# Idle transposes at the start, later and re-spread weight widening, and a scale ahead of the clamp, in a fused attention and mixer kernel on one core

## The chip, the cores and the metric

The kernel runs on one core of a Trainium2 chip. The metric is the device time of one execution in microseconds, taken as the median of several runs. The profile is one more execution, followed instruction by instruction. TensorE is called PE (its weight loads PEld), VectorE DVE, ScalarE ACT, GpSimd POOL, and the engine that issues most DMAs SP.

## The reference

Three layers in a row, on 4 batches of 576 tokens of 512 numbers (8 heads of 64), with weights that come in as 64-bit floats:

```python
q_p, k_p = phi(q_s), phi(k_s)                 # phi(x) = exp(h - max h)/sqrt(m), h = x @ omega.T - |x|^2/2
kv = einsum('bhsm,bhsd->bhmd', k_p, v); z = sum(k_p, axis=2)
x = einsum('bhsm,bhmd->bhsd', q_p, kv) / (einsum('bhsm,bhm->bhs', q_p, z)[..., None] + 1e-6)
h = maximum(x.T @ w_tok1, 0) @ w_tok2         # mixing over tokens
u = x + h.T
x = u + maximum(u @ w_ch1, 0) @ w_ch2         # 512 -> 1536 -> 512
u = x + real(fft(fft(x, axis=1), axis=2))
out = u + maximum(layernorm(u) @ w_ch1b, 0) @ w_ch2b   # 512 -> 2048 -> 512
```

## The kernel before

**Products.** Every product of full precision is three PE products of rounded parts (high by high, low by high, high by low). The program order of every engine is written out by hand, so an instruction that waits holds everything behind it on its engine, and a DMA that waits holds everything behind it on its queue.

**Attention** (`attention`, L781) runs in 72 slots, numbered n from 0, and seven more that finish; `order` (L691) holds one half tile of keys or of queries for each. Slots 0 to 9 are keys alone, 10 to 60 alternate keys and queries (so the last keys are in slot 60), and 61 to 71 are queries alone. In a slot PE makes six projections (`project`, L506); DVE takes their maximum (`feature`, L520); ACT makes the exponentials. Three slots later PE adds keys into the sums (`kv_add`, L540, eight products) or transposes queries (`turn`, L565, four). Five slots later it forms numerators (`numer`, L582, eight) that DVE divides (L595 to L602), and seven slots later it transposes the result (`turn_x`, L616). The mixing over tokens (`tok_mix`, L667 with 15 products and L680 with six, added by DVE in L683) is let in piece by piece once a batch is complete. SP loads the tile of a slot six slots ahead (`load`, L478 and L483), and ACT and POOL (keys of the first tiles also DVE) split it into parts four slots ahead (`split_in`, L493 and L494). Projections take their PSUM bank from four that rotate (`bank("A")`); the sums of keys take two that rotate (`bank("H")`).

**Widening** (`widen`, L319) turns a chunk of 64-bit weights into two 32-bit parts: a load into `stg` (L330), then DVE's clamp (`take`, L341), low bits (`rest`, L352), `size` (L356), `high` (L360), `low` (L364), `unit` (L368) and `scaled` (L372), with one ACT multiplication (`scale`, L348) between clamp and `size`. There are 32 chunks: four short ones for the mixing over tokens (640 and 576 columns), then 12 slabs and 16 halves of 1024 columns, which are stored to DRAM (`kept`) and fetched again where they are used. Two sets of buffers alternate, so the load of chunk i+2 overwrites `stg` of chunk i and waits for its `low`.

**Pacing** (`Side`, L202). `weave` (L383) puts the steps of all chunks in one list, each with a price in us of DVE (6.38 for a chunk of 1024). At the end of each slot `side.step(budget)` adds a budget to a credit (at most 4.6 is saved) and issues steps while the credit covers them. Loads and stores are put off by four slots (`side.later`), or are issued at once where a step needs them (`side.flush`). Budgets before: none in slots 0 and 1, 0 in slots 2 to 5, 1.2 in 6 to 9, 0.45 in 10 to 35, 1.2 from 36 on. After attention the channel blocks (`mlp`, L864) call `side.step` once per step of 24 PE products (L776 up, L898 down) with 3.9 in the first block, 1.2 in the second and 4.3 after; there the loads and stores go through POOL's queue without delay. ACT's `relu` (L860) and DVE's low part of it (L861) stand between up and down of a step, with the up product of the next step in between.

## Time and profile before

| what | us |
|---|---|
| median of 3 runs | 954.33 (954.07 to 955.66) |
| the profiled execution | 953.26 |
| its span, first to last instruction | 951.2 |
| PE busy in the span | 931.4 |
| DVE busy | 644.2 |
| ACT busy | 301.3 |

The span is 2.1 us shorter than the time of the same execution, and that execution is 1.1 us faster than the median. Attention's last piece on PE ends at 211.3 us; the blocks after it fill the rest. A PE that is busy is not always at its peak, because each product is drawn with its latency; where the text prices PE work it uses the distance from one start to the next.

### The profile page before, as it was taken

To read this page: it belongs to the slowest core of one execution; us is meant where nothing else is said; L and a number is where in the kernel's file an instruction comes from. 1 tells how busy PE (TensorE), PEld (TensorE's weight loads), DVE (VectorE), ACT (ScalarE), POOL (GpSimd) and SP (SyncE) were. 2 spreads that over 40 slices of the span, in tenths; PEclk is the share of its full clock that TensorE was granted. 3 is DMA by queue.
4 is the path that set the end of the run, shared out by engine and by line. 5 is a ranking of instruction groups with operands and counts; after the bars stand their busy time and mean duration, and the time that the engine had idled before them with its cause. 6 is when DMAs were issued, how large, how long until landed. Compare 5 with 4: busy or idle time off the path is not lost.

```text
span 951.2 us, 14064 instructions
## 1 busy us (share of the span) xinstructions
PE 931.4 (98%) x5344; PEld 829.7 (87%) x5344; DVE 644.2 (68%) x1270; ACT 301.3 (32%) x676; POOL 118.8 (12%) x110
## 2 busy tenths in 40 slices
PE   7999998989999999999999999999999999999998
PEld 7999898878889988888888888889899998899986
DVE  5987999985776687877864577667565457533342
ACT  5885765742122222212221212212311113311121
POOL 3353343321120122011000000000000000000000
PEclk9999999999999999999999999999999999999999
DMA  8665464388889386584155348739776756687764
GB/s 272 221 211 178 143 231 173 122 318 320 341 352 418 100 341 217 191 292 167 67 177 216 139 147 270 246 126 359 266 244 234 238 183 221 221 263 257 252 205 160
DMA packets 68257, 216.47 MB, mean 228 GB/s; under 512 B 5600, under 2 KB 14432, under 8 KB 54240
## 3 DMA queue, kind: packets, MB, share of 16 engines
q1 hardware_dynamic: 60992, 172.40, 51.9%
q0 software_dynamic: 7056, 43.06, 12.3%
q8 instruction: 42, 0.69, 0.3%
q14 instruction: 23, 0.19, 0.1%
q10 hardware_dynamic: 144, 0.13, 0.1%
HBM read 169.30 MB, written 42.47 MB: 223 GB/s over the span
## 4 chain that ended last, share of the span: by engine, by line
PE 89%; DVE 9%; ACT 1%; issue 0%; DMA 0%; DVEq 0%; ACTq 0%
PE H L776 22%; PE A L898 16%; PE A L1470 14%; PE H L1457 12%; PE A L1264 7%; PE A L506 4%; PE H L540 2%; PE N L582 2%; DVE mx L520 2%; PE A L667 1%; PE S L1077 1%; DVE cvo L364 1%; PE A L565 1%; PE S L1090 1%; DVE x L598 1%; DVE cvo L372 1%
## 5 line engine op out<-in xcount | busy, mean ns | idle before, releaser
L776 PE MATMUL H<-uh,w 128*128 128x512 f32 (+1 forms) x800 | 215.3, 355 | 2.1 <-DVE x L683 2.1
L776 PEld LDWEIGHTS H<-uh,w 128*128 128x128 f32 x800 | 136.5, 189 | 22.2 <-DVE x L683 2.3
L860 ACT ACTIVATE hh<-H 128x512 fp32r<-128x512 f32 (+1 forms) x92 | 49.0, 533 | 270.7 <-PE H L776 270.5
L776 PE MATMUL H<-ul,w 128*128 128x512 f32 (+1 forms) x304 | 113.7, 374 | 0.4 <-DVE ul L763 0.4
L898 PE MATMUL A<-hh,w 128*128 128x512 f32 (+1 forms) x480 | 108.7, 369 | 0.0
L861 DVE SCALAR_TENSOR_TENSOR hl<-H,hh 128x512 fp32r<-128x512 f32 (+1 forms) x92 | 55.8, 606 | 64.5 <-ACT hh L860 64.3
L1470 PE MATMUL A<-w2t,b 128*128 128x512 f32 x384 | 99.3, 394 | 0.0
L898 PEld LDWEIGHTS A<-hh,w 128*128 128x128 f32 x480 | 84.3, 189 | 15.0
L1457 PE MATMUL H<-b,w1t 128*128 128x384 f32 x480 | 91.5, 336 | 0.0
L1457 PEld LDWEIGHTS H<-b,w1t 128*128 128x128 f32 x480 | 85.0, 188 | 4.0 <-DVE tmp L1501 0.3
L1470 PEld LDWEIGHTS A<-w2t,b 128*128 128x128 f32 x384 | 70.6, 188 | 11.7
L524 ACT ACTIVATE f<-A,mx 128x128 f32<-128x128 f32 x204 | 58.9, 395 | 31.1 <-DVE mx L520 23.4
L776 PEld LDWEIGHTS H<-ul,w 128*128 128x128 f32 x304 | 57.4, 189 | 9.9 <-DVE ul L763 0.8
L898 PE MATMUL A<-hl,w 128*128 128x512 f32 (+1 forms) x240 | 59.2, 369 | 0.0
L1264 PE MATMUL A<-w,hh 128*128 128x512 f32 x192 | 50.5, 395 | 0.0
L520 DVE TENSOR_REDUCE mx<-A 128x4 f32<-128x512 f32 x70 | 47.6, 681 | 3.7 <-ACT f L524 2.2
L898 PEld LDWEIGHTS A<-hl,w 128*128 128x128 f32 x240 | 42.7, 189 | 7.6
L540 PE MATMUL H<-v,f 128*128 128x65 f32 x320 | 40.5, 272 | 0.4 <-ACT f L524 0.4
L540 PEld LDWEIGHTS H<-v,f 128*128 128x128 f32 x320 | 39.4, 193 | 0.8 <-ACT f L524 0.6
L1264 PEld LDWEIGHTS A<-w,hh 128*128 128x128 f32 x192 | 34.6, 189 | 6.1
L360 DVE SCALAR_TENSOR_TENSOR cvo<-cvy,cvo 128x1024 int32<-128x1024 int32 (+2 forms) x32 | 39.3, 1228 | 0.5
L1462 ACT ACTIVATE b<-tmp 128x384 fp32r<-128x384 f32 x16 | 8.4, 525 | 98.1 <-DVE tmp L1523 98.1
(261 smaller groups left out, 1703.4 us busy)
## 6 DMA issues: line engine op xcount, KB each, us to landing
w<-kept SPq DMA_DIRECT2D x60, 1024.0 KB, 6.8
w2t<-kept SPq DMA_DIRECT2D x55, 512.0 KB, 4.9
w1t<-kept SPq DMA_DIRECT2D x48, 512.0 KB, 5.0
stg<-in_wff_dram POOLq DMA_DIRECT2D x16, 1024.0 KB, 6.8
kept<-cvo POOLq DMA_DIRECT2D x13, 1024.0 KB, 7.3
stg<-in_wch_dram SPq DMA_DIRECT2D x9, 1024.0 KB, 6.1
kept<-cvo POOLq DMA_DIRECT2D x16, 512.0 KB, 7.7
kept<-so SPq DMA_DIRECT2D x16, 512.0 KB, 7.7
```

The costliest lines, as they stand in the source:

```text
L360: dve.scalar_tensor_tensor(out=st["h"], in0=st["y"].bitcast(I32), scalar=-0x80000000, in1=st["h"], op0=ALU.bitwise_and, op1=ALU.bitwise_or)
L506: pe.matmul(out=pj[:, p_ * 256:p_ * 256 + 256], lhsT=a[:, c, :], rhs=w, start=(n == 0), stop=(n == 2), skip_group_check=True)
L520: dve.tensor_reduce(out=mx, in_=p4, axis=AX.X, op=ALU.max, negate=True)
L524: act.activation(out=f[:, hh], in_=p4[:, hh], func=AF.Exp, bias=mx[:, hh])
L540: pe.matmul(out=kvp[b, g][:, hh * 65:hh * 65 + 65], lhsT=ft["k", i, g][:, hh, :], rhs=src["v", i, int(off > 0)][:, 4 * g + hh, :], start=( ...
L776: pe.matmul(out=hb[:, 0:n], lhsT=w(a, kk), rhs=u[:, kk, 0:n], start=(c == 0), stop=(c == 11))
L860: act.activation(out=hh, in_=hb[:, 0:n], func=AF.Relu)
L861: dve.scalar_tensor_tensor(out=hl, in0=hb[:, 0:n], scalar=0.0, in1=hh, op0=ALU.max, op1=ALU.subtract)
L898: pe.matmul(out=acc[i][:, 0:cols], lhsT=a[:, cs], rhs=v, start=(n == 0 and c_ == 0), stop=(n == NCH - 1 and c_ == 2))
L1264: pe.matmul(out=acc[t], lhsT=a[:, t * 128:t * 128 + 128], rhs=w, start=(n == 0 and c_ == 0), stop=(n == NFF - 1 and c_ == 2))
L1457: pe.matmul(out=to, lhsT=w[:, a, cs], rhs=v[:, q], start=(start and n == 0), stop=(n == 5), skip_group_check=True)
L1470: pe.matmul(out=acc[t], lhsT=h[n // 2][:, t * 128:t * 128 + 128], rhs=w[:, n % 2], start=(begins and n == 0), stop=(ends and n == 2))
```

## The change

The change has five edits. (1) After `projection()` PE runs 17 transposes of the identity into a bank of tag H before the first slot. (2) The values of a key tile are loaded one key tile later, so the first keys come ahead of values. (3) `scale` is now the first step of a chunk: ACT multiplies the strided words out of `stg` into `cvy` at no price, and DVE then clamps `cvy` in place with bounds that are scaled as well. In `weave` the scale of chunk i+1 is issued right after `size` of chunk i, ahead of `high`, `low` and `unit`; the clamp and the load of chunk i+2 keep their places. The `while` that forces an outstanding load moves from the clamp to `scale`. (4) `side.step` is first called in slot 8 and no longer in slot 2. (5) The budgets are 0 in slots 8 to 11, 0.6 in 12 to 25, 1.1 in 26 to 57, 0.3 in the eight slots 58 to 65 around the end of the keys (`alone` is 61) and 1.2 after; the first channel block gets 4.2 and no longer 3.9.

```diff
--- before.py
+++ after.py
@@ -27,13 +27,14 @@
 BLK = 512
 
 NWB = 3
+IDLE = 17
 NBLK = (NTOK + BLK - 1) // BLK
 
 BLOCKS = [0, NBLK - 1, *range(1, NBLK - 1)]
 
 
 
-SLOT0_US, SLOT1_US, SLOT_US, FIRST_US, SHORT_US, CH_US, FF_US, S_US, SAVED_US = 1.2, 0.45, 1.2, 3.9, 1.2, 4.3, 3.8, 1.6, 4.6
+SLOT0_US, SLOT1_US, ALONE_US, SLOT_US, FIRST_US, SHORT_US, CH_US, FF_US, S_US, SAVED_US = 0.6, 1.1, 0.3, 1.2, 4.2, 1.2, 4.3, 3.8, 1.6, 4.6
 
 
 NP = NFF // 2
@@ -329,30 +330,27 @@
             st["w"] = cv.tile([128, 2048], I32, tag=f"stg{k}", name="stg")
             side.queue.dma_start(out=st["w"][:, 0:2 * n], in_=src)
 
+        def scale():
+            while "w" not in st:
+                side.flush()
+            v = st["w"][:, 0:2 * n].rearrange("p (n w) -> p n w", w=2)
+            st["lw"], st["hw"] = v[:, :, 0], v[:, :, 1]
+            st["y"] = cv.tile([128, 1024], F32, tag=f"cvy{k}", name="cvy")[:, 0:n]
+            act.mul(out=st["y"], in_=st["hw"].bitcast(F32), mul=2.0 ** -112)
+
         def take():
-            while "w" not in st or k in busy:
+            while k in busy:
                 side.flush()
             busy.add(k)
-            v = st["w"][:, 0:2 * n].rearrange("p (n w) -> p n w", w=2)
-            st["lw"], hw = v[:, :, 0], v[:, :, 1]
-            st["y"] = y = cv.tile([128, 1024], F32, tag=f"cvy{k}", name="cvy")[:, 0:n]
             st["o"] = cv.tile([128, 2, 1024], F32R, tag=f"cvo{k}", name="cvo")
             st["h"], st["l"] = (st["o"][:, a, 0:n].bitcast(I32) for a in range(2))
-            dve.tensor_scalar(out=y, in0=hw.bitcast(F32), scalar1=HMAX, scalar2=-HMAX, op0=ALU.min, op1=ALU.max)
-            side.later(scale, 1)
-
-        def scale():
-
-            if "small" not in st:
-                st["small"] = True
-                act.mul(out=st["y"], in_=st["y"], mul=2.0 ** -112)
+            dve.tensor_scalar(out=st["y"], in0=st["y"], scalar1=HMAX * 2.0 ** -112, scalar2=-HMAX * 2.0 ** -112,
+                              op0=ALU.min, op1=ALU.max)
 
         def rest():
-            hw = st["w"][:, 0:2 * n].rearrange("p (n w) -> p n w", w=2)[:, :, 1]
-            dve.tensor_scalar(out=st["l"], in0=hw, scalar1=0x1FF, scalar2=None, op0=ALU.bitwise_and)
+            dve.tensor_scalar(out=st["l"], in0=st["hw"], scalar1=0x1FF, scalar2=None, op0=ALU.bitwise_and)
 
         def size():
-            scale()
             dve.tensor_scalar(out=st["h"], in0=st["y"].bitcast(I32), scalar1=3, scalar2=0x7FFFF000,
                               op0=ALU.logical_shift_left, op1=ALU.bitwise_and)
 
@@ -377,7 +375,7 @@
 
         f = n / 1024
         return (load, lambda: done(st, free)), [
-            (w * f, fn) for w, fn in ((0.68, take), (0.68, rest), (0.69, size), (1.21, high), (1.21, low), (0.69, unit),
+            (w * f, fn) for w, fn in ((0.0, scale), (0.68, take), (0.68, rest), (0.69, size), (1.21, high), (1.21, low), (0.69, unit),
                                       (1.22, scaled))]
 
     def weave(chunks):
@@ -386,13 +384,16 @@
         items = []
         for i, ((_, done), work) in enumerate(chunks):
             if not i:
-                items += [(0.0, chunks[c][0][0]) for c in range(2)] + work[:1]
-            items += work[1:6]
+                items += [(0.0, chunks[c][0][0]) for c in range(2)] + work[:2]
+            items += work[2:4]
             if i + 1 < len(chunks):
                 items.append(chunks[i + 1][1][0])
+            items += work[4:7]
+            if i + 1 < len(chunks):
+                items.append(chunks[i + 1][1][1])
             if i + 2 < len(chunks):
                 items.append((0.0, lambda i=i: side.later(chunks[i + 2][0][0])))
-            items.append(work[6])
+            items.append(work[7])
             items.append((0.0, lambda done=done: side.later(done)))
         return items
 
@@ -478,10 +479,17 @@
         sync.dma_start(out=t, in_=(kt if kind == "k" else qt)[:, i])
         src[kind, i] = t
         if kind == "k":
-            for part, row in enumerate([i] + [NT + c for c, j in enumerate(SPLIT) if j == i]):
-                t = ld.tile([128, H, D + 1], F32, tag="v", name="v", bufs=6)
-                sync.dma_start(out=t.rearrange("p h d -> p (h d)"), in_=va[row])
-                src["v", i, part] = t
+            values(i - 1)
+        if kind == "k" and i == NT - 1:
+            values(i)
+
+    def values(i):
+        if i < 0 or ("v", i, 0) in src:
+            return
+        for part, row in enumerate([i] + [NT + c for c, j in enumerate(SPLIT) if j == i]):
+            t = ld.tile([128, H, D + 1], F32, tag="v", name="v", bufs=6)
+            sync.dma_start(out=t.rearrange("p h d -> p (h d)"), in_=va[row])
+            src["v", i, part] = t
 
     def split_in(kind, i):
         t = src.pop((kind, i))
@@ -783,6 +791,7 @@
         at = {t: order.index(t + (int(t[0] == "q"),)) for t in tiles}
         late = {}
         n_all = len(order)
+        alone = max(n for n, x in enumerate(order) if x[0] == "k") + 1
 
         def at_slot(n, kind):
             return order[n][1:] if 0 <= n < n_all and order[n][0] == kind else None
@@ -828,9 +837,10 @@
             if 0 <= n < n_all:
                 feature(*order[n])
             results(n)
-            if n >= 2:
-
-                side.step(0.0 if n < 6 else SLOT0_US if n < 10 else SLOT1_US if n < 36 else SLOT_US)
+            if n >= 8:
+
+                side.step(0.0 if n < 12 else SLOT0_US if n < 26 else SLOT1_US if n < alone - 3 else
+                          ALONE_US if n < alone + 5 else SLOT_US)
             if fill and (len(fill) > 3 or n % 2 == 0):
                 fill.pop(0)()
             for fn in early[:3]:
@@ -839,6 +849,9 @@
 
     ctx.enter_context(tc.manual_schedule())
     projection()
+    idle = bank("H")
+    for _ in range(IDLE):
+        pe.transpose(idle[:, 0:128], ident, ident)
     side.rest += weave(tok_weights() + [slab(j) for j in range(NCH)]
                        + [w(p_) for p_ in range(NP) for w in (first, second)])
     attention()
```

## Rows read from the trace of the kernel before

**Rows 1.** Page, part 1: busy time, share of the span and instructions of each engine.

```profile
PE 931.4 (98%) x5344; PEld 829.7 (87%) x5344; DVE 644.2 (68%) x1270; ACT 301.3 (32%) x676; POOL 118.8 (12%) x110
```

**Rows 2.** Stretches cut at first projections: length, busy (count), PEclk, DMA share, GB/s.

```profile
5.19:11.97 6.78, 6.78 (x32) 6.56 (x33) 5.21 (x8) 3.50 (x11) 3.87 (x3) 1.00 0.88 293
11.97:32.13 20.16, 19.76 (x169) 19.25 (x168) 16.04 (x26) 13.61 (x39) 6.83 (x5) 1.00 0.57 197
...
84.72:144.92 60.20, 58.31 (x460) 55.63 (x458) 56.90 (x109) 38.98 (x98) 23.81 (x15) 1.00 0.52 180
144.92:185.84 40.92, 36.51 (x286) 34.18 (x286) 39.85 (x84) 26.78 (x67) 14.08 (x9) 1.00 0.38 142
185.84:211.33 25.49, 21.95 (x156) 19.98 (x154) 22.65 (x56) 13.75 (x26) 7.39 (x6) 1.00 0.79 294
211.33:282.98 71.65, 71.65 (x337) 60.36 (x338) 50.91 (x69) 14.03 (x20) 11.35 (x14) 1.00 0.88 334
```

**Rows 3.** Chain of waits: start, duration, engine, tile, line, count of products.

```profile
182.51 3.49 PE H L667 x15
186.00 0.71 PE A L506 x6
186.71 0.44 PE A L565 x4
187.15 0.84 PE N L582 x8
...
193.21 0.84 PE H L680 x6
```

**Rows 4.** Stretches cut at maxima (L520): length, PE, PEld, DVE, ACT, POOL busy.

```profile
33.71:55.09 21.38, 21.38 (x191) 21.38 (x190) 20.48 (x49) 19.18 (x54) 10.87 (x8) 1.00 0.90 262
55.09:75.11 20.02, 20.02 (x178) 20.02 (x178) 16.61 (x44) 18.65 (x53) 10.02 (x8) 1.00 0.65 225
86.16:148.16 62.00, 59.61 (x467) 56.59 (x467) 59.54 (x115) 40.63 (x102) 23.81 (x15) 1.00 0.53 186
148.16:188.26 40.10, 36.20 (x287) 34.17 (x287) 38.94 (x83) 26.52 (x65) 15.14 (x10) 1.00 0.36 130
```

**Rows 5.** Same stretches, only instructions on tile cvo (six of seven widening steps): DVE busy.

```profile
55.09:75.11 20.02, 4.00 (x7) 0.00 (x0) 1.00 0.65 225
86.16:148.16 62.00, 26.33 (x23) 0.00 (x0) 1.00 0.53 186
148.16:188.26 40.10, 17.00 (x14) 0.00 (x0) 1.00 0.36 130
```

**Rows 6.** Same stretches, only the clamp (L341), the seventh step: DVE busy.

```profile
55.09:75.11 20.02, 0.68 (x1) 1.00 0.65 225
86.16:148.16 62.00, 5.29 (x4) 1.00 0.53 186
148.16:188.26 40.10, 1.36 (x2) 1.00 0.36 130
```

**Rows 7.** Timeline of the start: start, duration, engine, line, operation, out<-in [idle before].

```profile
1.23 0.29 POOL masks.py:199 TENSOR_SCALAR_AFFINE_SELECT ident<-ident 128x128 f32<-128x128 f32 x1
...
7.93 0.62 ACT L493 CAST kh<-ks 128x512 fp32r<-128x512 f32 x1 [2.79 <-DMA ks<-in_kt_dram]
...
9.92 0.41 PE L506 MATMUL A<-om_h,kl 128*128 128x256 f32 x1
10.14 0.41 PE L506 MATMUL A<-om_h,kh 128*128 128x256 f32 x1
...
12.18 0.28 PE L506 MATMUL A<-om_l,kh 128*128 128x256 f32 x1
12.29 0.28 PE L506 MATMUL A<-om_h,kl 128*128 128x256 f32 x1
```

**Rows 8.** Page, part 6: a DMA issue, its size and its time to landing.

```profile
stg<-in_wch_dram SPq DMA_DIRECT2D x9, 1024.0 KB, 6.1
```

**Rows 9.** Waits: who waited for whom, us in total, times, longest.

```profile
ACT hh L860 <- PE H L776: 270.5, 81, 6.8
```

## The prediction

> **What bounds the kernel now.** The page comes first: PE is busy for 98% of the span, DVE for 68% [rows 1]. A busy PE can still be waiting inside its drawn latencies, so I then cut the span by slots [rows 2] and priced each stretch by the distances between products that the chain of waits shows where nothing holds PE: six projections 0.71 us, four transposes 0.44, eight numerators (and, with the same shape, eight key sums) 0.84, fifteen L667 products 3.49, six L680 products 0.84 [rows 3]. The price is what PE needs; the rest of the length is lost.

> From 211.33 on PE is busy all the time [rows 2], so widening that moves there costs nothing while it keeps out of PE's way. Attention is where time can be won. In slots 4 to 14 the 169 products need 18.9 of 20.2 us: 1.2 lost. In slots 15 to 35 PE is busy for the whole length [rows 4] and loses nothing. In slots 38 to 57 the 460 products need 56.9 of 60.2: 3.3 lost. In slots 58 to 70 the 286 products need 34.0 of 40.9: 6.9 lost [rows 2, 3]. Where PE loses, DVE is at 96 to 97% [rows 4], and a large part of its work is widening: 26.3 + 5.3 = 31.6 of 59.5 us in slots 38 to 57 and 17.0 + 1.4 = 18.4 of 38.9 in slots 58 to 70 [rows 4 to 6]. There DVE is the bound, by work that nobody needs yet.

> The price of a credit follows. 20 slots at 1.2 are 24 credits and took 31.6 us, 1.32 us each; 13 slots at 1.2 are 15.6 and took 18.4, 1.18 each; the ten slots 26 to 35 at 0.45 are 4.5 and took 4.7, 1.04 each [rows 5, 6].

> **Part 1, the idle transposes.** `ident` is ready at 1.52. [...] PE had been busy since 5.19 without a break [rows 2]. [...] Both ends: 0, if the rise stays, and 3.1, if all 32 products of the stretch ran at the high level (24 at 0.118 and 0.84 are 3.7, not 6.8). ACT waits 2.8 us for the third key tile until 7.93 [rows 7], and it now comes one value tile earlier in the queue; that keeps the gain alive. I take 1.6. [...]

> **Part 2, no widening before slot 12.** The 1.2 us lost in slots 4 to 14 follow the 4.8 credits of slots 6 to 9, which go away. I take 0.7 of it (0 to 1.2), because ACT now holds the first scale in slot 8, where the load has only just been issued.

> **Part 3, slots 12 to 35: the cost.** In slots 15 to 25 DVE has 0.9 us idle in 21.4 [rows 4] and gets 11 x 0.15 = 1.65 more credits, 2.1 us at 1.3: 1.2 too much. In slots 26 to 35 it has 16.6 of work, 4.7 of it widening [rows 4 to 6], so 11.9 of other work. The new budgets are 11 credits: 11.4 to 14.5 us, a total of 23.4 to 26.5 in a length of 20.0, thus 3.4 to 6.5 too much. PE does not lose all of it. DVE may fall behind before the banks run out: slot 38's maximum starts 1.4 us after its projection, slot 58's 3.2 [rows 2, 4], so at least 1.8 is free. That leaves 2.8 to 5.9 lost where nothing was lost; in slots 36 and 37, with 30 products of L667, DVE catches up. I take 4.0, nearer to the middle; the ends are 1 and 7.

> **Part 4, slots 38 to 57.** 22 credits at 1.32 are 29.0 us in place of 31.6, and with the 27.9 of other work DVE has 56.9, exactly PE's need. I take the difference of DVE's work, 2.5 won (0 to 3.3).

> **Part 5, slots 58 to 70.** 8 x 0.3 + 5 x 1.2 = 8.4 credits at 1.2 are 10.1 us in place of 18.4; with 20.6 of other work DVE has 30.7, under PE's need of 34.0. The 6.9 lost should shrink to about 1.4, which I leave for places where DVE is late within a slot: 5.5 won (3.0 to 6.9). About 8 credits in all go to the channel blocks, where DVE is busy for 50.9 of 71.7 us [rows 2]; the 3.3 credits more of the first block fit there. If that cover failed they would cost 8 to 10 us. The last slots keep their budget, and DVE stays the bound there (22.7 busy of 25.5 [rows 2]): 0, between 1.5 lost and 1 won. I take 0.3 lost for the next point.

> **Part 6, the scale ahead of the clamp.** The work is the same: one multiplication on ACT, one clamp on DVE. No row shows ACT reading strided words. DVE's clamp reads them now and costs 1.3 us on average in slots 38 to 57 (0.68 elsewhere [rows 6]), so I take nothing for the stride, 0.3 us either way for each of 32 chunks, none of it on the path. What does change is who waits for the load. The buffer is free after `low` of two chunks before; from there to `scale` lie `unit`, clamp, `scaled`, `rest` and `size`, 4.0 credits, where there were 7.1 up to the clamp. At 1.1 per slot of 3 us that is 10.8 us, and a load lands in 6.1 [rows 8]: hidden. Around slots 28 and 29, with chunks of 576 columns and slots of 2 us, it is only 4 to 5, and ACT stands for 2 to 4 us with exponentials and copies behind it; DVE is too late there anyway, so it is inside the 4.0. In the channel blocks 4.0 credits are about one step of 6 us, less than the load with its issue, so ACT stands in many steps, and `relu` of the next step behind it. ACT waits 270.5 us over 81 waits for PE there, 3.3 each [rows 9], and the product after `relu` comes one up product later; that covers most. I take 0.7 lost (0 to 3).

> **Sum.** 1.6 + 0.7 - 4.0 + 2.5 + 5.5 - 0.3 - 0.7 = 5.3 us won. Against the profiled execution (953.3, span 951.2) that is 948.0 with a span of 945.9; against the median, 1.1 higher, 949.0.

> **The rivals.** (a) The transposes do not move the rise: without the 1.6 it is 950.6. For it speaks the rule above, against it only that PE is seen working; 0.27. (b) Slots 12 to 35 are overfull: in slots 15 to 25 both DVE and ACT have under 2.3 us idle [rows 4], and at 1.6 us for a credit, as contention in such slots could make it, slots 26 to 35 would have 29.5 us of DVE work in 20.0. The loss is then 8 to 9 in place of 4, and the time 953.5; 0.16. (c) Slower: the load is reached by SP only at its place in SP's order, in the same slot as `scale`, because a wait for an input buffer stands ahead of it. Each of the seven slabs of slots 29 to 70 then holds ACT for 6.1 us [rows 8], of which 1.8 is free as above; I take half of the other 4.3 as covered by the three slots between exponentials and sums: 7 x 2.2 = 15 lost, 964. It decides once a load issues within 6 us of its `scale`, in slots of 3 us less than two slots ahead. Against it: SP's input loads run six slots ahead of their use. 0.10. (d) The forecast, 0.45; the last 0.02 is left for others.

> **How the numbers follow.** Something within 0.2%, 1.9 us, is about what cannot be told from no change. The forecast's own range, from the ends of its terms, is 944 to 953. (a) lies inside it, (b) ends it at 955, and (c) is left out: 943.8 to 955.5 leaves a fifth out. Faster by over 0.2% (below 952.4): nearly all of (d), nine tenths of (a), a third of (b): 0.73. Within: 0.15. Slower: (c) and the tail of (b), 0.12.

> **What would show it.** Products of 256 columns 0.11 apart by 8.5 us (part 1). First projection of slot 15 some 2.3 earlier than 32.13, of slot 38 then 1 to 2 later than 84.72, with PE waiting on DVE or ACT between 45 and 75; DVE idle in slots 58 to 65, and the first up product some 6 earlier than 211.33. ACT waiting on DMA at the line of `scale`, in single cases of some us. A span from 211 to the end longer than now by over 2 us, or slots 26 to 35 longer than 26 us, would make the prediction wrong.

## The result, and the profile after

| what | before | after |
|---|---|---|
| median of ten runs each, us | 954.29 (953.32 to 959.28) | 963.92 (956.99 to 966.18) |
| profiled execution, us | 953.26 | 963.25 |
| its span, us | 951.2 | 961.5 |

The ratio is 1.0075, with a 95% interval of 1.0049 to 1.0100 (the quotient of the two medians is 1.010). The change makes the kernel slower by 0.5 to 1.0%; the forecast was 949.0, with 955.5 as the upper end of its range. After's runs spread with the mean granted clock of PE: 956.99 us at 0.998, 966.18 at 0.988. The profiled execution has 0.987 and is 10.0 us longer than that of before.

To see where, both spans are cut at the same places, the first projection of a slot or the first product of a block. Each length below is the difference of two starts in the timelines.

| stretch | before | after | won (+), lost (-) | forecast |
|---|---|---|---|---|
| start to slot 4 | 11.97 | 9.91 | +2.06 | +1.6 |
| slots 4 to 14 | 20.16 | 18.86 | +1.30 | +0.7 |
| slots 15 to 25 | 20.71 | 20.68 | +0.03 | -4.0, with the next row |
| slots 26 to 37 | 31.88 | 41.57 | -9.69 | |
| slots 38 to 57 | 60.20 | 64.26 | -4.06 | +2.5 |
| slots 58 to 70 | 40.92 | 34.59 | +6.33 | +5.5 |
| slot 71 to the first block | 25.49 | 25.81 | -0.32 | -0.3 |
| block 0 | 79.82 | 82.77 | -2.95 | -0.7, with the next rows |
| block 1 | 36.93 | 36.85 | +0.08 | |
| block 2 | 66.00 | 68.99 | -2.99 | |
| the rest | 557.09 | 557.19 | -0.10 | |

Four of the forecast's terms are there: parts 1, 2 and 5, and the last slots. The rows that went wrong are slots 26 to 57 and blocks 0 and 2. Where block 0 starts is the second step of the first block; the first products of the block start earlier, between the last pieces of attention.

The same stretches of after as in [rows 2] and [rows 4]: length, busy time (count) of PE, PEld, DVE, ACT and POOL, PEclk, DMA share, GB/s.

```profile
9.91:28.77 18.86, 18.86 (x168) 18.86 (x168) 11.80 (x20) 15.11 (x46) 7.30 (x6) 1.00 0.76 259
49.45:91.02 41.57, 38.83 (x253) 36.63 (x252) 33.75 (x69) 26.24 (x71) 13.29 (x10) 0.84 0.63 219
91.02:155.28 64.26, 61.24 (x460) 58.91 (x458) 56.01 (x108) 39.04 (x97) 23.55 (x15) 0.95 0.46 166
155.28:189.87 34.59, 34.59 (x287) 33.91 (x286) 31.43 (x78) 26.08 (x66) 12.97 (x9) 1.00 0.27 96
215.68:298.45 82.77, 81.74 (x384) 68.71 (x385) 59.10 (x83) 17.65 (x26) 12.15 (x16) 0.98 0.84 322
335.30:404.29 68.99, 67.09 (x289) 53.78 (x288) 53.77 (x77) 15.63 (x26) 14.87 (x18) 1.00 0.70 244
```

The column to look at is the third from the right. The granted clock is 0.84 in slots 26 to 37, 0.95 in 38 to 57 and 0.98 in block 0; before it was 1.00 in every attention stretch of [rows 2]. Slots 58 to 70 have lost their stalls: PE is busy for all 34.59 us, and DVE has 3.2 us idle where it had 1.1 [rows 2].

Cut finer, the lower clock (granted 0.50; from 64.17 to 64.81 projections start 0.21 to 0.22 us apart, and 0.12 from 78.58 on, at 1.00) lies in three pieces. The rows are pairs, the stretch ahead and the stretch at the lower level, with the columns as above.

```profile
59.90:63.35 3.45, 2.06 (x17) 1.78 (x15) 3.31 (x12) 2.12 (x8) 0.00 (x0) 1.00 0.82 305
63.35:77.00 13.65, 12.58 (x58) 12.29 (x58) 11.16 (x22) 8.65 (x24) 4.24 (x3) 0.50 0.70 258
...
114.55:117.96 3.41, 1.93 (x14) 1.56 (x14) 3.34 (x9) 1.58 (x5) 0.00 (x0) 1.00 0.75 308
117.96:124.79 6.83, 6.83 (x35) 6.83 (x34) 4.32 (x8) 4.43 (x11) 3.16 (x3) 0.50 0.15 41
...
213.50:216.95 3.45, 1.27 (x6) 1.05 (x6) 3.45 (x7) 0.00 (x0) 0.67 (x2) 1.00 0.70 247
216.95:220.36 3.41, 3.41 (x10) 2.64 (x9) 3.26 (x5) 1.27 (x2) 0.49 (x1) 0.50 0.90 348
```

In the stretch ahead of each fall PE has stood idle for 1.4, 1.5 and 2.2 us, while DVE was busy for nearly all of it. So PE waited for DVE, as the forecast expected in the first two, and then worked at a granted clock of 0.50 for much longer than it had waited, which the forecast did not have at all. Slots 26 to 37 show the two shares: of the 9.69 us lost PE stood idle for 2.7 (41.57 - 38.83, where before it had no idle time), and it was busy for 7.0 longer with the same products (38.83 against 31.88), about half of the 13.65 us at the lower level.

The first pause in the timelines of PE, DVE and ACT, with the releaser of an idle time in brackets, and DVE's and PE's timelines at the second:

```profile
54.15 1.55 DVE L354 TENSOR_SCALAR cvo<-cvy 128x576 int32<-128x576 int32 x1
...
57.27 1.46 DVE L358 SCALAR_TENSOR_TENSOR cvo<-cvy,cvo 128x576 int32<-128x576 int32 x1
...
59.33 0.68 DVE L528 TENSOR_REDUCE mx<-A 128x4 f32<-128x512 f32 x1
...
60.04 1.14 ACT L532 ACTIVATE f<-A,mx 128x128 f32<-128x128 f32 x4 [1.05 <-DVE mx L528]
...
61.23 0.39 PE L514 MATMUL A<-om_h,qh 128*128 128x256 f32 x1 [1.09 <-ACT f L532]
```

```profile
106.98 1.79 DVE L366 TENSOR_SCALAR cvy<-cvo 128x1024 int32<-128x1024 int32 x1
...
110.38 1.33 DVE L347 TENSOR_SCALAR cvy<-cvy 128x1024 f32<-128x1024 f32 x1
...
117.57 0.39 PE L514 MATMUL A<-om_h,qh 128*128 128x256 f32 x1 [1.11 <-DVE rd L603]
```

At the first place ACT's exponentials (L532) are late because the maxima that they need stand behind widening on DVE. At the second PE's longest wait is for DVE itself (L603), which stands behind widening too. At both places two widening steps are stretched. Those of 1024 columns took 1.79 and 1.33 us, and the median of either kind is 0.69; those of 576 columns took 1.55 and 1.46, where the other pair of that size took 0.45 and 0.75. A sum of 512 columns ran on POOL beside each of the four. Of the 196 widening steps of 1024 columns in this trace, the 175 with no such sum beside them took 0.71 us at most (the four short kinds) or 1.23 (the three long ones); of the 21 others 14 took longer than that, up to 1.79 and 1.95 (POOL's spans are rough). That POOL is the cause was not tried.

### The profile page after: what moved, and what is told of

The parts are those of the page before. It is cut to its first block, busy times and chain, and to the rows that moved or that the text cites. A ratio compares the mean times of both kernels' runs of the same rounds, so it can differ in the third digit from the quotient of the medians.

```text
span 961.5 us, 14144 instructions
## 1 busy us (share of the span) xinstructions
PE 942.7 (98%) x5361; PEld 839.6 (87%) x5361; DVE 644.0 (67%) x1270; ACT 302.9 (31%) x676; POOL 117.7 (12%) x112
## 4 chain that ended last, share of the span: by engine, by line
PE 84%; DVE 8%; DMA 5%; issue 2%; ACT 0%; POOL 0%; DVEq 0%; ACTq 0%; POOLq 0%; SPq 0%
PE H L784 19%; PE A L1483 14%; PE H L1470 12%; PE A L911 11%; PE A L1277 7%; PE A L514 4%; PE H L548 3%; PE N L590 3%; DMA stg<-in_wff_dram 3%; PE A L675 1%; PE A L573 1%; PE S L1090 1%; DMA w<-kept 1%; PE S L1103 1%; DVE cvo L370 1%
## 5 line engine op out<-in xcount | busy, mean ns | idle before, releaser
L532 ACT ACTIVATE f<-A,mx 128x128 f32<-128x128 f32 x204 | 58.6, 382 | 27.3 <-DVE mx L528 24.6
L339 ACT ACTIVATE cvy<-stg 128x1024 f32<-128x1024 f32 (+2 forms) x32 | 35.3, 1103 | 96.9 <-DMA stg<-in_wff_dram 73.0
L528 DVE TENSOR_REDUCE mx<-A 128x4 f32<-128x512 f32 x70 | 47.5, 682 | 8.6 <-PE A L514 7.1
```

Of the source, the lines that this page charges most:

```text
L339: act.mul(out=st["y"], in_=st["hw"].bitcast(F32), mul=2.0 ** -112)
L528: dve.tensor_reduce(out=mx, in_=p4, axis=AX.X, op=ALU.max, negate=True)
L532: act.activation(out=f[:, hh], in_=p4[:, hh], func=AF.Exp, bias=mx[:, hh])
```

## The experiments

Four theories were set against each other. **A**: the loss is ACT standing at `scale` for a load. **D**: it is DVE, overfull in slots 26 to 37 by the new budgets, as rival (b) had it. **C**: what costs is the clock that falls after PE's pause, whatever made the pause. **S**, formed after the first four runs: the first block is as long as the storing of the last slab is late, so that widening which leaves attention comes back there. Medians of before on the same chip were 953.87 in the first four runs, 953.79 in the next four, 954.04 in the next three and 952.63 in the last.

### Scale or budgets

**Clamp first again**, all else as in after. A says that attention recovers.

```diff
-            items += work[4:7]
-            if i + 1 < len(chunks):
-                items.append(chunks[i + 1][1][1])
...
+            dve.tensor_scalar(out=y, in0=hw.bitcast(F32), scalar1=HMAX, scalar2=-HMAX, op0=ALU.min, op1=ALU.max)
+            side.later(scale, 1)
```

> The changed kernel with the clamp ahead of the scale again and the old order of steps (the load is then first waited for by the clamp, 3.1 credits later); start, budgets and order of loads as in the change. Theory D: the lower clock around 63 to 77 stays, slot 38 near 90, and only what the channel blocks lost (5 us) comes back: about 958. Theory A: no stretch of lower clock at all, slot 38 at 85 to 86, no loss in the blocks: 948 to 951.

Measured: 956.58 (952.76 to 960.66, ten runs), ratio 1.0014 [0.9999, 1.0030]. Stretches of its profiled execution (960.66, the slowest of the ten): slots 26 to 37, the lower clock, block 2.

```profile
49.47:90.81 41.34, 38.83 (x253) 36.66 (x252) 33.92 (x69) 25.77 (x72) 13.52 (x10) 0.83 0.66 206
63.35:77.00 13.65, 13.29 (x62) 12.73 (x61) 11.36 (x24) 9.81 (x28) 3.79 (x3) 0.50 0.76 270
335.32:401.32 66.00, 66.00 (x289) 54.09 (x288) 55.07 (x79) 16.73 (x27) 16.39 (x18) 1.00 0.72 255
```

Attention is as long as in after, with the clock falling at the same times. A does not explain slots 26 to 57. Block 2 is back at 66.00: the early `scale` costs 3.0 us there. In five of the ten runs the mean clock is 0.995 or more; four of them lie between 952.76 and 953.81 and the fifth (0.996) at 957.66, where after's one run at 0.998 took 956.99. The ratio's interval includes 1: this kernel can't be told from before.

**Scale alone**, on before.

```diff
-            items += work[1:6]
+            items += work[2:4]
             if i + 1 < len(chunks):
                 items.append(chunks[i + 1][1][0])
+            items += work[4:7]
+            if i + 1 < len(chunks):
+                items.append(chunks[i + 1][1][1])
```

> The kernel before with the scale ahead of the clamp and the new order of steps alone; no idle transposes, old budgets, old order of loads. Theory A: ACT waits on DMA at the line of the scale for 50 us or more in sum, PE pauses, and 4 to 10 us are lost: 958 to 964. Theory D: with budgets of 0.45 the waits are hidden in attention, only the channel blocks lose 2 to 5: 956 to 959, and the granted clock stays at its higher level.

Measured: 969.52 (966.76 to 970.03, four runs), ratio 1.0153 [1.0132, 1.0174]. Attention is 0.9 us shorter, block 0 is 11.9 longer and block 2 5.5. From its waits (engine, tile and line, who was waited for: us, times, longest), its stretches and its chain:

```profile
ACT cvy L338 <- DMA stg<-in_wff_dram: 89.9, 12, 12.4
```

```profile
210.47:302.18 91.71, 83.83 (x384) 70.00 (x385) 56.89 (x81) 16.57 (x25) 11.67 (x16) 0.94 0.83 318
289.03:295.86 6.83, 3.98 (x9) 3.14 (x10) 4.00 (x6) 3.00 (x6) 0.11 (x1) 0.50 0.51 216
```

```profile
273.17 16.97 DMA stg<-in_wff_dram
```

One load took 16.97 us to land, where the median of these loads is 6.8 on the page of this kernel and of before. ACT stood for it with `relu` behind, PE waited 6.7 us for `relu` in one piece, and the clock fell within that wait and stayed down for 6.83 us. The time is above what both theories gave. By the same table cut at the blocks, ACT stands 48.8 us for five loads in block 0 and 43.2 for six in block 2; in after it is 31.2 for five and 44.7 for six. The wait is in both kernels, and what it costs PE depends on which loads come late.

**Before's early budgets** in after, scale still first.

```diff
-            if n >= 8:
+            if n >= 2:
 
-                side.step(0.0 if n < 12 else SLOT0_US if n < 26 else SLOT1_US if n < alone - 3 else
+                side.step(0.0 if n < 6 else 1.2 if n < 10 else 0.45 if n < 36 else SLOT1_US if n < alone - 3 else
```

> The changed kernel with one thing undone: widening starts in slot 6 again, with the budgets of before up to slot 35 (1.2 in 6 to 9, 0.45 in 10 to 35); 1.1, 0.3 and 1.2 behind it as in the change, and the scale ahead of the clamp stays. Theory D (DVE is overfull in slots 26 to 35, PE pauses there and the granted clock falls to its lower level at 63): no stretch at the lower clock before slot 36, the first projection of slot 38 at 82 to 84 in place of 91.0, and some 7 us less in all, about 957. Theory A (ACT stands in the scale for a load that has only just been issued, and PE pauses behind it): the scales are still early, so a stretch of lower clock stays in or near slots 26 to 48, slot 38 at 87 or later, and 961 or more.

Measured: 961.05 (959.50 to 962.33, four runs), ratio 1.0070 [1.0050, 1.0089]. Stretches: slots 26 to 37, 38 to 57, block 0.

```profile
52.81:85.60 32.79, 32.55 (x252) 30.81 (x252) 26.13 (x64) 25.52 (x72) 12.36 (x9) 1.00 0.53 184
85.60:143.95 58.35, 57.27 (x459) 55.60 (x458) 54.49 (x108) 38.97 (x97) 22.14 (x15) 1.00 0.51 173
205.93:297.25 91.32, 86.30 (x385) 72.05 (x386) 57.36 (x81) 16.86 (x25) 11.83 (x15) 0.93 0.83 313
```

The clock stays at 1.00 through slots 26 to 57, as D has it. Slot 38 starts at 85.60, between what D and A gave, and the whole takes what A gave, though its loss lies elsewhere. Slots 38 to 57, whose budgets are those of after, now win 1.85 us over before, where after lost 4.06: the forecast's +2.5 for them was nearly right, and what turned it in after seems to come with the slots ahead, whose budgets alone differ. The first block starts 5.4 us earlier than before, and is 11.5 longer. So what is won in attention is lost again, in a place that the forecast called free.

**The start alone**, on before: 17 transposes and the later values.

```diff
+    idle = bank("H")
+    for _ in range(IDLE):
+        pe.transpose(idle[:, 0:128], ident, ident)
...
+            values(i - 1)
```

> The kernel before with the idle transposes and the later values alone. Both theories: products of the first slots at the higher clock from about 6 us on, slot 4 some 2 us earlier than 11.97. What is left of it at the end tells whether attention keeps a gain from its start: 952 to 953 if it does, 954.3 if DVE and ACT, not PE, set the slots after it.

Measured: 958.11 (953.95 to 960.73, ten runs in two groups: four at 953.95 to 954.36 with a mean clock of 0.998, six at 957.44 to 960.73 with 0.991 to 0.993), ratio 1.0034 [1.0015, 1.0053]. Its profiled execution is of the first group. Slots 4 to 14 in it:

```profile
9.99:31.52 21.53, 19.74 (x168) 19.22 (x168) 15.41 (x27) 14.55 (x43) 7.37 (x6) 1.00 0.61 216
```

Slot 4 starts at 9.99, 1.98 us before [rows 2], so the start's gain is there without the rest of the change. Slots 4 to 14 then take 21.53 where they took 20.16 [rows 2], and 0.61 is left: PE, now earlier, runs into the 4.8 credits of slots 6 to 9. The start only pays when that widening is moved too; parts 1 and 2 belong together. The median is above both expected times. What the runs of the second group lose was not profiled.

### The clock

**Fillers in after**: ten idle transposes ahead of the projections in slots 29 to 32 and 46 to 48, around the two pauses. That adds 70 products, 7.7 us of PE at 0.11 [rows 3].

```diff
+        if at_fill(kind, i, g):
+            for _ in range(10):
+                pe.transpose(pj[:, 0:128], ident, ident)
```

> The changed kernel with more work for PE: ten idle transposes ahead of the projections of slots 29 to 32 and 46 to 48, into the bank that the projection takes; 70 in all, 7.7 us at the higher clock. Theory C (what was lost in slots 26 to 58 is the lower clock that follows PE's pauses, and not DVE's lateness itself): the clock stays at its higher level through 63 to 77 and 118 to 125, the first projection of slot 38 comes at 84 to 87 in place of 91.0, of slot 58 at 145 to 149 in place of 155.3, and the whole is 954 to 958 in place of 963, although PE has more to do. Theory D alone (DVE's lateness is the loss, the clock only goes with it): no gain, 964 to 971.

Measured: 959.74 (959.04 to 961.04, four runs), ratio 1.0064 [1.0047, 1.0081], against 963.92 and 1.0075 [1.0049, 1.0100] for after. The intervals overlap, so these runs don't show that the whole became faster, and it lies between what C and D alone gave. What they show is by stretch. Slots 26 to 37 and 38 to 57, and the two stretches that had the lower clock in after:

```profile
49.36:85.81 36.45, 36.28 (x293) 34.81 (x292) 34.21 (x69) 25.91 (x71) 13.84 (x10) 1.00 0.68 234
85.81:148.94 63.13, 60.88 (x489) 58.83 (x488) 56.06 (x108) 38.91 (x97) 23.03 (x15) 1.00 0.51 179
63.35:77.00 13.65, 13.48 (x120) 13.28 (x120) 13.30 (x29) 10.68 (x31) 5.64 (x4) 1.00 0.72 266
117.96:124.79 6.83, 6.83 (x63) 6.83 (x61) 5.42 (x12) 4.80 (x14) 1.59 (x1) 1.00 0.67 237
```

In these slots PE has more work and takes less time. From 63.35 to 77.00 PE makes 120 products in place of 58. Slots 26 to 37 take 36.45 in place of 41.57, although 40 fillers (4.4 us) are among them, and C holds for these 5.1 us. The 4.6 us still lost over before are about the fillers' own work (PE is busy for 36.28 of the 36.45), so this run doesn't say what DVE's lateness alone costs: at most 4.6. After's ten runs point the same way without fillers: the one with a mean clock of 0.998 lies 2.7 us above the median of before, where the median of the ten lies 9.6 above. The start of the first block comes 6.4 us earlier than in after, and 2.0 earlier than before; block 0 then has 83.50.

### The first block

**The quiet slots alone**: clamp first and before's early budgets, so only the start, the budgets from slot 36 on and the first block's 4.2 differ from before.

```diff
+            if n >= 2:
+                side.step(0.0 if n < 6 else 1.2 if n < 10 else 0.45 if n < 36 else SLOT1_US if n < alone - 3 else
...
+            side.later(scale, 1)
```

> The changed kernel with two things undone: the clamp is ahead of the scale again and widening has the early budgets of before (1.2 in slots 6 to 9, 0.45 to 35). What is left: idle transposes, later values, 1.1 in slots 36 to 57, 0.3 in 58 to 65, 4.2 in the first block. By the stages seen so far the first up product is then 5 to 6 us earlier than in the kernel before. Theory S (the first block pays for the widening that was moved, because its last slabs are stored too late to be fetched in time): the first block is 5 to 9 us longer than the 79.8 of before, and the whole comes out at 953 to 957. If moved widening is free: 948 to 950.

Measured: 960.64 (954.10 to 965.27, ten runs), ratio 1.0074 [1.0049, 1.0098]. The first block starts 5.3 us earlier than before and block 0 takes 91.88, 12.1 longer, without the early scale: in block 0 the scale is not the cause. PE's waits there, and the chain of waits:

```profile
PE H L784 <- DMA w<-kept: 6.4, 3, 2.8
PE H L784 <- DVE x L691: 2.9, 1, 2.9
```

```profile
265.82 9.55 DMA kept<-cvo
...
275.43 8.88 DMA w<-kept
...
284.35 4.60 PE H L784 x12
```

The last slab is stored from 265.82 and fetched again from 275.43; PE's last step needs it at 284.35. That is 18.5 us behind the store, and the store comes 59.8 us after the block's start, where before had 45.1. The slabs are not all of the 12.1: PE waits 6.4 us for them, and the clock is at the lower level for 10.24 us of the block in three pieces (from 206.54, 274.80 and 285.04), half of which is 5.1. The piece at 206.54 follows the 2.9 us for which PE waited for L691 ahead of the block, so it is not the slabs'.

**A larger budget for the first block**, 5.2 in place of 4.2 in the kernel above.

```diff
-    ..., 0.6, 1.1, 0.3, 1.2, 4.2, ...
+    ..., 0.6, 1.1, 0.3, 1.2, 5.2, ...
```

> The run before this one with one size changed: 5.2 in place of 4.2 for the first block, so that its last slab is stored about where it was. Theory S: the first block is back at 80 to 82 us and the whole at 948 to 951, faster than the kernel before. If not the slabs but something else lengthens the first block, it stays at 85 or more.

Measured: 955.11 (953.85 to 960.01, ten runs), ratio 1.0022 [1.0007, 1.0038]. The last store begins 55.2 us after the start of the block, and block 0 takes 86.67: 5.2 of the 12.1 come back. By what was expected this speaks against S, which gave 80 to 82. But the store did not come back to 45.1 either, so S was only half tried here.

**Still more moved there**: 0.3 in the last seven steps of attention too, 5.5 for the first block.

```diff
-                          ALONE_US if n < alone + 5 else SLOT_US)
+                          ALONE_US if n < alone + 5 or n >= n_all else SLOT_US)
```

> As the run before, with 0.3 in place of 1.2 in the last seven steps of attention too (where the chain of waits shows 7 us of widening on DVE) and 5.5 for the first block. If DVE is the bound in these steps, the first up product of the second step comes 3 to 5 us earlier still; if slabs are then late, the first block gives back 2 to 5. Expected: 945 to 949.

Measured: 961.52 (960.22 to 965.75, four runs), ratio 1.0086 [1.0061, 1.0111]. The first block starts 11.2 us earlier than before, the last store comes 74.0 after that start, and block 0 takes 98.05. PE's waits in it:

```profile
PE H L784 <- DMA w<-kept: 12.4, 3, 5.4
```

Last store after the block's start against block 0's length: 45.1 and 79.8 (before), 53.5 and 82.8 (after), 55.2 and 86.7, 59.8 and 91.9, 74.0 and 98.0. The length grows with the store, as S says, but the scale alone, with 47.5 and 91.7, doesn't fit: there PE waits for `relu`. What fits every kernel is an estimate of two terms, PE's idle time in the block plus half of the time at the lower clock: 2.7 of the 2.95 lost in after, 6.5 of 6.9, 11.5 of 12.1 and 19.2 of 18.2 in the three kernels with the later stores, 13.0 of 11.9 in the scale alone. So, by this estimate, a late slab cost its wait and, behind it, a fall of the clock (in the quiet slots alone 6.4 us of waits, and the pieces at the lower clock from 274.80 and 285.04).

### Putting it together

**Eight quiet slots, the rest given to long slots**: before with 3.0 in slots 36, 37, 52 and 53, in which 15 products of L667 keep PE busy, and 0.3 in slots 58 to 65.

```diff
-                side.step(... SLOT1_US if n < 36 else SLOT_US)
+                side.step(... SLOT1_US if n < 36 else 3.0 if n in (36, 37, 52, 53) else 0.3 if 58 <= n < 66 else SLOT_US)
```

> The kernel before (no idle transposes, clamp first, old order of loads) with its budgets changed only from slot 36 on: 3.0 in slots 36, 37, 52 and 53, where PE has fifteen products of L667 to do, 0.3 in slots 58 to 65, 1.2 elsewhere; the first block keeps 3.9. By the credits the same slabs are done at the end of attention as before (s7, with s8 begun). Theory S with theory C: slots 58 to 70 some 5 us shorter, no pause in slots 26 to 48, the first block at 80 to 82 us: 948 to 951, faster than the kernel before. If DVE's work in slots 36, 37, 52 and 53 is not covered, slot 58 comes 2 to 4 us later and the gain is gone: 953 to 955.

Measured: 954.75 (953.21 to 956.43, ten runs), ratio 1.0001 [0.9981, 1.0021]. Slots 58 to 70 take 34.46 where they took 40.92, and block 0 79.81 with the last store 45.1 after its start. Slots 38 to 57 take 67.84 in place of 60.20: the 3.0 in slots 52 and 53 seem to be too much, and the clock is at the lower level from 139.2 to 146.0.

**The same with a quiet tail** and 5.2 in the first block:

```diff
+                ... else 0.3 if 58 <= n < 66 or n >= n_all else SLOT_US)
```

> The run before this one with 0.3 also in the last seven steps of attention and 5.2 in place of 3.9 in the first block; its last slab is stored one step later by the credits. Attention ends 9 to 11 us earlier than in the kernel before; the first block takes 82 to 88. 945 to 951: faster than the run before this one if the slabs still come in time, slower if the first block waits for two of them.

Measured: 952.29 (951.28 to 956.79, ten runs), ratio 0.9984 [0.9963, 1.0005]. The first block starts 3.2 us earlier than before, the last store comes 51.2 after, and block 0 takes 83.88. Not to be told from no change.

**The eight quiet slots with the start**, its early widening spread as 0.6 over slots 4 to 11.

```diff
+                side.step(0.0 if n < 4 else 0.6 if n < 12 else SLOT1_US if n < 36 else ...
```

> e11_quiet8 with the idle transposes and the later values, and the 4.8 credits of slots 6 to 9 spread over slots 4 to 11 (0.6 each), so that PE does not run into one lump of widening. If the start's gain survives: slot 15 at 29.5 to 31 in place of 32.13, no lower clock between 15 and 40, and 1 to 2.5 us less than e11_quiet8. If PE, now earlier, pauses in slots 9 to 15 as in e5_quiet_only (lower clock from 25.6 to 29.0), the runs spread over 5 us or more and the median is 2 us or more above e11_quiet8.

Measured: 949.49 (948.47 to 952.20, ten runs), ratio 0.9946 [0.9925, 0.9968]. Slot 15 starts at 29.10, 3.0 earlier than before, and this time the gain reaches slot 38 (82.21, 2.5 earlier). The lower clock from 136.7 to 143.5 is still there.

**Without the lump in slots 52 and 53** (1.2 there, 4.6 in the first block):

```diff
-                ... 3.0 if n in (36, 37, 52, 53) else 0.3 if 58 <= n < 66 else SLOT_US)
+                ... 3.0 if n < 38 else 0.3 if 58 <= n < 66 else SLOT_US)
```

> e12_quiet8_start with 1.2 in slots 52 and 53 in place of 3.0, and 4.6 in place of 3.9 in the first block for the credits that are then missing. In e11, e10 and e12 the clock fell for 6.8 us behind slot 53 (136.7 to 143.5 in e12) and slots 38 to 57 took 66 to 68 us in place of 60.2. If the lump of widening in 52 and 53 made PE pause there, that fall is gone, slots 38 to 57 take 58 to 61 us, and the whole is 943 to 947. If it has another cause, the fall stays and the whole is 949 or more.

Measured: 948.96 (948.20 to 950.12, five runs), ratio 0.9960 [0.9946, 0.9973]. Slots 38 to 57, 58 to 70, the tail, and block 0 of its profiled execution:

```profile
82.17:143.25 61.08, 58.69 (x460) 55.83 (x458) 56.86 (x109) 39.43 (x98) 23.84 (x15) 1.00 0.59 199
143.25:178.82 35.57, 35.00 (x285) 34.03 (x286) 32.84 (x79) 26.01 (x66) 12.42 (x9) 1.00 0.21 75
178.82:206.14 27.32, 23.48 (x157) 21.49 (x155) 23.77 (x52) 12.77 (x25) 7.23 (x6) 0.94 0.79 284
206.14:285.93 79.79, 79.79 (x385) 67.54 (x385) 61.45 (x86) 17.37 (x26) 14.15 (x18) 1.00 0.94 353
```

Slots 38 to 57 no longer have the fall, which speaks for the lump as its cause, but the whole is above the 943 to 947 expected for that, and it can't be told from the kernel before it (0.9946 [0.9925, 0.9968]). This and the one before it beat both kernels. The first block starts 5.2 us earlier than before and is no longer than before (79.79; last store 47.4 after the start). So two ideas of the change, the start and the eight quiet slots, pay together, with the early widening spread over slots 4 to 11 and the other put into slots 36 and 37. Neither was faster than before alone (958.11 and 954.75). What the change paid for them with was not good.

## Why the prediction was wrong

**Part 1, the start: right.** 2.06 won where 1.6 was taken. PE's timeline of after at the start:

```profile
1.58 3.88 PE L854 MATMUL H<-ident 128*128 128x128 f32 x17 [1.58 <-POOL ident masks.py:199]
5.36 0.38 PE L514 MATMUL A<-om_h,kh 128*128 128x256 f32 x1
5.58 0.28 PE L514 MATMUL A<-om_l,kh 128*128 128x256 f32 x1
...
6.31 0.28 PE L514 MATMUL A<-om_h,kh 128*128 128x256 f32 x1
6.43 0.28 PE L514 MATMUL A<-om_l,kh 128*128 128x256 f32 x1
```

The projection at 5.58 takes 0.28 us, as do those from 6.31 on, which start 0.12 apart, as they do from 78.58 on at a granted clock of 1.00: the upper level. Before, projections took 0.41 until 10.14, after 5 us of them from 5.19 on, and 0.28 at 12.18 [rows 7]. The granted clock reads 1.00 in both stretches of before [rows 2], so the level at the start is read from the products themselves. In after one projection lies between the transposes and the upper level, and in the start alone three (0.28 to 0.30 from 6.36 on), so the transposes moved the rise, from 0.41 to 0.28 us a projection. Rival (a) is out: no run shows a rule by which transposes leave the rise where it was, and these rows, like the start alone, show that they moved it. Nor does a run show the 1.6 us as such, which was the author's estimate; in its place the start alone showed 1.98 and the change 2.06.

**Part 2: right.** 1.30 won, 0.7 taken, a little over the upper end of 1.2. The start alone shows what would have happened without it.

**Part 3: the step that failed.** "PE does not lose all of it" took a pause of PE to cost its own length, less what the banks hide. The cost of DVE's overrun was sized well: cut at the maxima as in [rows 4], DVE has 25.71 us of work in slots 26 to 35, where 23.4 to 26.5 were forecast, and PE stands idle for 2.7 us in slots 26 to 37, where 2.8 to 5.9 were to be lost. What the forecast lacks is the 13.65 us at the lower level behind the pause, in which PE's own work became 7.0 us longer. That makes 9.69 in place of 4.0, and the bound of 7 was too low for the same reason. The same stretches of after as in [rows 4], slots 26 to 35 and 38 to 57:

```profile
52.39:82.54 30.15, 27.41 (x184) 26.47 (x183) 25.71 (x54) 21.37 (x56) 11.43 (x9) 0.77 0.65 222
92.45:157.21 64.76, 61.74 (x465) 59.41 (x464) 57.33 (x112) 39.21 (x100) 23.55 (x15) 0.95 0.48 170
```

"In slots 36 and 37 DVE catches up" came true: they take 11.04 us as before (11.05), at the upper clock. But PE has its own 11 us of work there, so what was lost ahead of them can't be won back. The size of rival (b), 8 to 9, came out, but not by its mechanism: it had 29.5 us of DVE work at 1.6 us for a credit, and the 11 credits took 14.2 of the 25.71, 1.3 each. Stretched steps are there, ahead of both pauses (1.79 and 1.33 us at the second, where the median is 0.69); that contention stretches them was not shown.

**Part 4: the mechanism right, the sign turned.** +2.5 forecast, -4.06 measured, +1.85 with the same budgets in the run with before's early budgets. DVE has 57.33 us of work by the cut of [rows 4], where 56.9 were forecast and 59.54 stood before. The clock was at 0.50 from 117.96 for 6.83 us: PE is busy for 2.9 us longer than before (61.24 against 58.31) and idle for 1.1 longer. Why PE pauses there in after and not in that run is not settled; the stretched steps at 106.98 and 110.38 are what the trace shows ahead of it.

**Part 5: right.** +6.33 against +5.5 (3.0 to 6.9), and DVE has 31.43 us of work against 30.7. The last slots came out at -0.32 against -0.3.

**"The 3.3 credits more of the first block fit there": failed.** DVE did have room, but room was the wrong question. The widening that stays behind attention includes the slabs that the first block itself consumes, and each goes to DRAM and back before PE can use it. Block 0 lost 2.95: 1.70 of it are its first 12 products at the lower clock (4.44 us, where the next 12 take 2.74), behind a wait of 2.42 us for DVE (L691) ahead of the block, and 1.03 PE's wait for the last slab. The chain of after:

```profile
215.68 4.44 PE H L784 x12
...
223.83 2.74 PE H L784 x12
...
269.21 8.15 DMA kept<-cvo
277.40 9.00 DMA w<-kept
286.45 3.04 PE H L784 x12
```

The forecast named the price of a failed cover as "8 to 10 us", and put no chance on it. In after the cover failed in part, since much of the widening was done early, in slots 12 to 35, at the price of part 3. In the run with before's early budgets block 0 lost 11.5 us: PE waits 5.0 for slabs, and 13.65 us of the block are at the lower clock. The "about 8 credits" that go to the blocks are 6.5 by the budgets.

**Part 6: mis-sized.** 0.7 was taken (0 to 3) and block 2 lost 2.99, all of it given back by the clamp first. In the table of waits of after, ACT's longest wait at `scale` is 10.3 us:

```profile
ACT cvy L339 <- DMA stg<-in_wff_dram: 73.0, 11, 10.3
ACT cvy L339 <- DMA stg<-in_wch_dram: 13.2, 3, 6.7
```

The 3.3 us of cover for each wait [rows 9] was a mean, and single loads landed far later than that. Of these 86.2 us, 86.0 lie behind 215, so rival (c), which had ACT standing in attention, is out as a mechanism, although its time, 964, is the one measured. The forecast read the clamp's 1.3 us in slots 38 to 57 as the price of strided words. After's clamp reads none and still takes 1.26 us there on average (three steps), with a median of 0.69 in both kernels, so these traces show no such price.

**The signs given in the forecast.** Slot 15 started 3.36 earlier (2.3 said). Slot 38 started 6.3 later (1 to 2 said), the first block 4.35 later (6 earlier said), and the part behind it became 5.96 longer, over the 2 us that were to make the forecast wrong; so is the length of slots 26 to 35, 30.5 where 26 was the limit. The range of 944 to 953 "from the ends of its terms" is narrower than these ends, which add up to 939.8 and 962.8; the 963.92 lie outside them too.

Open: the ten runs of after and those of four other kernels spread over 6 to 11 us with the mean clock, so it seems that falls come and go from run to run. One profiled execution shows where they can lie, not how often. A fall at 200.7 to 204.1 is left even in the last kernel.

## What to carry to other kernels

Where PE is the bound, background work on the vector engines has to be paced so that PE does not stand still: price a pause at its length plus what PE loses while its clock is down afterwards (2.7 and 7.0 us in slots 26 to 37 of after), and read the granted clock behind each pause (in before PE stood for 4.4 us in slots 58 to 70, at 1.00 [rows 2]). Before calling work free in a later stage, look up who consumes its result there and by when, through the store and the fetch (8.15 and 9.00 us for the last slab of after), and not only whether the engine has idle time. An instruction that waits for a load does not belong ahead of a step of the critical loop in an engine's program order, even if its mean wait seems covered: in the scale alone ACT stood for loads for up to 12.4 us, and PE waited 6.7 us in one piece for the `relu` behind such a wait.
